# Second head's probability tiles turned by a DMA round over DRAM and VectorE's 32x32 transposes, with a new order of issue

## The chip, the cores and the metric

The kernel runs on one core of a Trainium2 chip. The metric is the device time of one execution in microseconds, from the program's start to its end. Five engines work side by side, each through its own list of instructions in the order in which they were issued: TensorE (matmuls and transposes, PE in the profile, PEld for its weight loads), VectorE (DVE), ScalarE (ACT), GpSimd (POOL) and SyncE (SP), which here only issues DMAs.

## The reference

Eight batches of eight heads of attention with a threshold, and a gated MLP behind it:

```python
# q, k, v: 8 x 8 x 576 x 64; x: 8 x 576 x 512
scores = scale * q @ k^T
thresh = max(scores, axis=-1) - tau
attn   = exp(where(scores >= thresh, scores, -1e9) - max); attn /= attn.sum(-1) + 1e-9
x      = heads of (attn @ v) side by side
h      = gelu(x @ w_in); u, v = halves of h
v_n    = (v - mean) / sqrt(var + 1e-6) * g_ln
gated  = u * (w_sg @ v_n + b_sg)
out    = x + gated @ w_out
```

## The kernel before, in words

Two heads make a pair, so there are 32 pairs, numbered n from 0, four a batch. A pair's 576 rows are cut into four tiles of 128 rows for each head and one tile that holds the last 64 rows of both. For each of the nine tiles TensorE makes the scores (L835, in a split of two float32r parts that adds up to full precision; L810 for pairs 0 to 3), VectorE takes the negated maximum (L844), GpSimd the threshold (L850), ScalarE the exponential (L871), and VectorE sets to zero what lies below the threshold and sums the row (L878). The result is the tile `p`, rows of queries by columns of keys, with head 0 in the first 512 columns and head 1 in the last.

The value product needs the keys on the partitions, so every 128x512 piece of `p` is turned: TensorE makes four 128x128 transposes into a PSUM bank (`transposes`, L538 by way of `turn`), with the data as weights and the identity as the moving operand, and ScalarE copies the bank into the tile `pt` (`place`, L1001). For pairs 4 to 30 head 1's four tiles go another way: a DMA copies the piece of `p` into a tile `m` of the type float32r (`move`, L887), and TensorE turns that (`turn_moved`, L541), where one pass an element is enough. The values then multiply `pt` in two parts of 256 and 320 columns (`values`, L1027), both heads into one bank. The row sums go through DRAM to lie along the columns (`ld`, L947 to L954), and VectorE scales (L1036).

Four finished pairs feed one batch's MLP: matmuls at L1126, each group of four followed by work of the other engines (L1105 to L1328), and a store (L1334).

What sets the order: all steps are collected in a list `plan`, and a table of numbers (`PLACES`) gives each step its place. A planner runs through the steps in that order with a price for each instruction and gives each PSUM result a free bank. The steps are then issued in that order, so each engine gets its instructions in it, and SyncE its DMAs, which it issues one after the other, each when what it waits for has come. A new DMA also waits for the eighth one before it. There are two rooms for `m`, two for `p`.

Of the kernel before, what the change touches and what calls it, by code (L numbers as in the profile page):

```python
# [14 lines left out]
F32 = mybir.dt.float32  # L15
# [19 lines left out]
PLACES = (  # L35
    "c-qZa3v^ZGmA>D9&b{ZJ`@YG2<^7NlNFWd1fdGO6Di&)Mb+lAkbzC#*npxAaUB#tst=h*b>ddqbOO{%7Xlt!)t!<}8+X@A-JmewBoA3q`z+iY9"
    "k~81_Pog|RAP^jna?id0+5f-y{`R*YCmzS~c-;Rx|H;k0cYf>q>TymHX#Yf@y-V5lQ+Ay4`N<y7NqbIRJxSO(d8w;yZSvDOb=${}Pdnwzr(Hkr"
    "oT|y`g|j_foZa5t?laH!^zdx-^4XqK?RF1z;G8aY#{O;=&h9{mp3}(Jjh=27y4BNmN(%JE{B!x^oZ*jidOGy79;XvG=ThkLoK4U9;^tg151dOI"
    "pC0++oR2@wNy5&>;&y5M=|w$V1n{&1;`AU-oll(yXX^2s<JgnCsB@NuGqSM@+`6LIxfS;yf1Dop(_=kd^36GCU+4xm=REm#0bxI@9?z$qKWE10"
    "Q>+KhS!jGlh@Fe$!8y$LT!cSe^=;>T)1@c=c+P@bw~6cYoClth>ZsFQy7YwC=fKVBQG7fX;?D()g*}=>x}V>ii>{;2X>;$HRr36QJKbRBUi&?#"  # L40
    "_ss6Eb3H#z!0ATBxxiDLi!tx4BA3*0ryIw6$5p4Ni=V3F=MT!IK=Cu`xaR_~Isc>E|Nk6!dg@2-z|g&h&t#5YiuixFbKG-*aqI=hdlHs&g4jFm"
    "IK7cmM!Tb4yD?!Oi<!z%cjIf<1&#(ni9VZ$s<Fzkec);W2mYbWOu=U#n_^7A_1fQmTV<jj-f0{d@_tS~3X~ywXmXpm3(0*+Zz?loYspZU@#c6="
    "!?aP;zJl2|KAJ!ArrKEYo7bSYZtB~0bp{YnkquA%=5YgA$VTGM2cNwoo`}FM#gfUp`-4|9g8Os(HI$k_Fp;{ad}O?Y+maYFX?R-{@FNPtGwwik"
    "IRyf@#~K0=e0ank2Q05DTmxSasV4ga8z$nhjj-VlBl}&OdMhJu!W%8ZAuJ8SXO6<c0yKgW3I9d}QH(bH7KobJ8Q_48GI@ks3bsFYgjNMhtaqrd"
    "IJgnVxNPRcRs%+v8MNNxG6vx9{OpU}sRcX&gR!gv%{0mM;R9F^1ta{E5Hc!}!fnq7fgJu<_T$3L(L)rs(%1~sAH%`$hkO>SP|K*>NEz7br@u&U"
    "rzLTozsly9zSxk9BL*#wU^hRLF!1XdlmiOp+CrjANz~T(9v8bqM$UR3S!{lQCcz|(1N=;Sfx~>L^05wf$jZ&e^9C$jjyG?>Vhf6R?xAcEPncz)"
    "K;mMh12m#U0pBZ&n@)T`mQAb9%+1=zXZ~C?nAA@Yp;qypJwz>%SYe!c2dxSLvj7c%54eIxFI0SVHU9Tb%%N<+Ux5XRo(-o*bG6Q#G!L5)&!SV`"
    "xi^2zHgfUuy<E3T@SdncDSh0`Z)TQ+Fqk4LJ}^KQuELvQEhZBfh7*x~ST`Df;$9!ETQB+w8KG6w1ytEzB#RC|cLf#PmbG?_(T-<ka^2?*H9-I^"
    "!H3wH=GQu`6%0^`4cJPJ-tpESZLwqmcKha8JauB=)oMPJp!dTv>Or2-YHd#nc%{KAa`@J#`ch9t>5Qki^yq9#hSO@JDW{AlOiet+?t^!A)GF0V"
    "oFIOIfn*jXbIP&R_pVq!(pXT8?Sg{097|;-hU3N|t622-cI5+`O7CKFmZpAlBMLEm3)cgwIO)ou55;CB3uXn@SpriHj;ie>oxci;X^9Gt!a@8G"  # L50
    "zeH{eJ$+5`4+<e425LP<ifr406nCWut&Qek@A&@6-(?Sb;cn|A3~!-Cuo!E2SRNVEtQc>^ZH60W5GC;qXk(?})5E3^p%N|L6=B*`hK>0=7N%hg"
    "#4>{%OK@YO)>A;P;?5`Q%jnOT^h3`uK3DCco_Gq|Buq@SEhH*kD`TJ}^YYLFN+3J|ztZs;g!R}%SN$XLRzgTmm7m8i6gOYSQm~ha2vqmkW7gtF"
    "*XE#P>&@vW9;2T7=1Lp_L_>DeVS_rTHR3pJi8FDUu}3K<Iu*Z^`1r?Q6W)%Ikkm6I@Or>(vr&tM25V^<WgC%8vC-IvDVRQaGS3)3V8)M0hg*bK"
    "-coHoh{|p(=iMmHo9~0(u@@)!J7Z#}{EpU>AdCt!)9_-I>@s3TiH?t5NQ8HwO2kSJB!Rc_5cLGE{JP*aPVzL&d^d&0g@F%rE`&?5K1|cpK*G2Q"
    "NEnluHOfFFg(GMMAEmIbH1q-$+N^T#2n0Dek=&@`lgw()#)JpQUkjssN_6^bhT~KivL1$}9n#b#Tn+dbSK>)R9?~gn)q|CiO`rmP>kY44*M<Za"
    "=sX>bH^jCYhHHb?lL%W1*-v~wg!>j27ytZU>Ceb!p>ay+MPAoa%WeU(Kr8kJhcQd(u^BCm%;%Xgqml{ycg3uqg5Q=wvO8n2?ijG`Fj{=Af|^Y("
    "sHy&$H<jVCE#<ZAucV$5zdT4w($klrB$w2kK#rzehy?=JZdxB%WAHkBt-eqtNjOJ^j@i@j>v0j*9p%L+{8h2L<{=PTP6VVL98oqFKE|g`W&aod"
    "g}7aQ#EpLgm%_a7GdGIHIHc|cQ4`t5PJ%$#?7LWajy}jvzV7FffI2(~FA*-NT(u+2_{5kutN01;Wm3bYUH6pexwm!8HQp2G$M_iD8Z6QN3}Mh&"
# [24 lines left out]
)
LAST_SCALE, SIGMA, SPREAD = 0.55, 1.155, 0.7
# [1331 lines left out]
```

## Time and profile before

| what | us |
|---|---|
| three timed runs | 961.38, 961.41, 962.68 (median 961.41) |
| the profiled execution, from its first to its last instruction | 959.4 |
| TensorE busy in it | 936.8 |
| VectorE, ScalarE, GpSimd busy | 663.8, 667.1, 564.4 |
| the sixteen DMA engines, share of the span | 45.6% |

For the profiled execution the profile gives the span alone; the median of the runs lies 2.0 us above it, which is what goes on around the first and last instruction. Busy time of TensorE is the union of its instructions, and these are pipelined: one begins before the one ahead of it has ended. How much room an instruction takes on TensorE is the distance from its start to that of the next. The share of busy time is a mean over stages; the pairs with moved tiles make one long stage in the middle, with the weights' preparation and pairs 0 to 3 ahead of it and the last batch's MLP behind it.

### The profile page before, as it was taken

Reading aid. Unit: us, or ns where it says so; the run is one execution under the profiler, and the core shown is the slowest. Engines: PE = TensorE matmul, PEld = TensorE weight load, DVE = VectorE, ACT = ScalarE, POOL = GpSimd, SP = SyncE. Lnnn points to the kernel's source line nnn. Section 1 sums busy time; section 2 is a strip of 40 time slices with the busy share of each in tenths; the row PEclk is TensorE's granted clock in tenths of the full one; section 3 lists DMA queues with packets and bytes.
Section 4 is the critical chain, followed back from the end, with each engine's and each line's share of the span. In section 5 each row is a group of like instructions: output and inputs, shape, how many; then the busy total and the mean of one; then the engine's idle time right before and its main releaser. Section 6 shows DMA issues by size and latency. Waiting matters only on the chain.

```text
span 959.4 us, 20206 instructions
## 1 busy us (share of the span) xinstructions
PE 936.8 (98%) x6822; PEld 800.2 (83%) x6822; DVE 663.8 (69%) x1407; ACT 667.1 (70%) x1395; POOL 564.4 (59%) x997
## 2 busy tenths in 40 slices
PE   7999999999999999999999999999999999999998
PEld 4555889987798888998888898888889888898898
DVE  7899975767777567666786568766677757765451
ACT  5987886767875677665777677766787567764552
POOL 5865665555644577446763557536675366644467
PEclk9999999999999999999999999999999999999999
DMA  8353145465545553555445554456535455341001
GB/s 299 111 143 99 61 123 148 149 185 158 149 129 151 158 147 118 136 162 167 136 133 158 153 153 141 133 142 185 156 119 153 141 160 155 98 127 52 20 7 50
DMA packets 75791, 128.74 MB, mean 134 GB/s; under 512 B 16948, under 2 KB 25383, under 8 KB 75688
## 3 DMA queue, kind: packets, MB, share of 16 engines
q1 hardware_dynamic: 75688, 127.45, 45.6%
q8 instruction: 54, 0.88, 0.4%
q14 instruction: 49, 0.40, 0.1%
HBM read 46.40 MB, written 9.56 MB: 58 GB/s over the span
## 4 chain that ended last, share of the span: by engine, by line
PE 77%; ACT 7%; DVE 7%; DMA 3%; POOL 3%; issue 2%; SPq 0%; POOLq 0%; DVEq 0%; ACTq 0%
PE all_banks L1126 36%; PE all_banks L1027 14%; PE all_banks L835 14%; PE all_banks L538 8%; PE all_banks L541 3%; ACT p L871 2%; DVE nm L844 2%; DVE p L878 1%; DMA m<-p 1%; ACT pt L1001 1%; POOL ot L1331 1%; DMA qz<-qhi 1%; PE all_banks L810 1%; DVE gt L1112 1%; ACT vv L1218 1%
## 5 line engine op out<-in xcount | busy, mean ns | idle before, releaser
L871 ACT ACTIVATE p<-all_banks,nm 128x576 f32<-128x576 f32 x256 | 184.6, 742 | 92.5 <-DVE nm L844 90.6
L844 DVE TENSOR_REDUCE nm<-all_banks 128x1 f32<-128x576 f32 x288 | 208.7, 751 | 52.5 <-PE all_banks L835 43.3
L878 DVE SCALAR_TENSOR_TENSOR p<-all_banks,nm,p 128x576 f32<-128x576 f32 x256 | 204.2, 813 | 48.3 <-POOL nm L850 27.2
L1001 ACT ACTIVATE pt<-all_banks 128x512 f32<-128x512 f32 (+1 forms) x320 | 163.9, 554 | 19.4 <-PE all_banks L538 11.4
L835 PE MATMUL all_banks<-ks,qst 128*128 128x288 f32 x560 | 157.1, 314 | 1.4 <-ACT pt L1001 0.6
L850 POOL TENSOR_TENSOR nm<-columns,nm 128x1 f32<-128x1 f32 x288 | 55.0, 195 | 147.6 <-DVE nm L844 134.5
L1027 PE MATMUL all_banks<-pt,rv 128*64 128x256 f32 (+1 forms) x1024 | 137.8, 411 | 0.0
L835 PE MATMUL all_banks<-kl,qz 128*128 128x288 f32 x448 | 123.6, 295 | 0.0
L538 PE MATMUL all_banks<-ident_r,p 128*128 128x128 f32 x720 | 115.7, 276 | 3.1 <-DVE p L878 2.3
L835 PEld LDWEIGHTS all_banks<-ks,qst 128*128 128x128 f32 x560 | 102.1, 188 | 14.6 <-issue 6.9
L1126 PE MATMUL all_banks<-wsh,z 128*128 128x288 f32 (+2 forms) x512 | 113.4, 298 | 0.3 <-DVE uu L1109 0.3
L1027 PEld LDWEIGHTS all_banks<-pt,rv 128*64 128x64 f32 x1024 | 69.5, 136 | 48.6 <-issue 6.1
L538 PEld LDWEIGHTS all_banks<-ident_r,p 128*128 128x128 f32 x720 | 84.9, 141 | 20.0 <-issue 6.5
L1126 PEld LDWEIGHTS all_banks<-wsh,z 128*128 128x128 f32 x512 | 85.1, 188 | 2.4 <-issue 1.4
L835 PEld LDWEIGHTS all_banks<-kl,qz 128*128 128x128 f32 x448 | 84.5, 189 | 0.2
L1126 PE MATMUL all_banks<-xh,wih 128*128 128x288 f32 (+2 forms) x256 | 77.0, 301 | 0.2 <-ACT ot L1328 0.2
L1126 PE MATMUL all_banks<-gh,woh 128*128 128x288 f32 (+2 forms) x256 | 76.6, 300 | 0.0
L1126 PE MATMUL all_banks<-xl,wih 128*128 128x288 f32 (+2 forms) x256 | 76.0, 297 | 0.0
L1126 PE MATMUL all_banks<-xh,wil 128*128 128x288 f32 (+2 forms) x256 | 75.8, 296 | 0.0
L1126 PE MATMUL all_banks<-gh,wol 128*128 128x288 f32 (+2 forms) x256 | 75.8, 297 | 0.0
L1126 PE MATMUL all_banks<-wsl,z 128*128 128x288 f32 (+2 forms) x256 | 75.7, 297 | 0.0
L1126 PE MATMUL all_banks<-gl,woh 128*128 128x288 f32 (+1 forms) x240 | 70.7, 296 | 0.0
(147 smaller groups left out, 2202.2 us busy)
## 6 DMA issues: line engine op xcount, KB each, us to landing
m<-p SPq DMA_DIRECT2D x108, 256.0 KB
rk<-in_kT SPq DMA_DIRECT2D x32, 320.0 KB
rv<-in_vP SPq DMA_DIRECT2D x32, 320.0 KB
ks<-khi SPq DMA_DIRECT2D x56, 160.0 KB
rq<-in_qT SPq DMA_DIRECT2D x31, 288.0 KB
qz<-qhi SPq DMA_DIRECT2D x56, 144.0 KB
qst<-qhi SPq DMA_DIRECT2D x56, 144.0 KB
qst<-rq SPq DMA_DIRECT2D x56, 144.0 KB
```

The costliest lines, as they stand in the source:

```text
L538: nc.tensor.transpose(out, x, ident_r.bitcast(F32))
L541: nc.tensor.transpose(out.bitcast(F32R), x, ident_r)
L810: nc.tensor.matmul(st["s", h, i][:, a, 0:HALF], st["q"][rows, qo:qo + P], st["k"][rows, lo:lo + HALF], start=True, stop=True)
L835: nc.tensor.matmul(sc[:, a, 0:HALF], w, x, start=(j == 0), stop=(j == len(terms) - 1))
L844: nc.vector.tensor_reduce(nmax, st["s", h, i][:, :, 0:HALF], AX.XY, ALU.max, negate=True)
L850: nc.gpsimd.tensor_tensor(thr, toff, st["nm", h, i], ALU.subtract)
L871: nc.scalar.activation(target(h, i), st["s", h, i][:, :, 0:HALF], AF.Exp, bias=st["nm", h, i])
L878: nc.vector.scalar_tensor_tensor(dst, st["s", h, i][:, :, 0:HALF], st["thr", h, i], dst, ALU.is_ge, ALU.mult, accum_out=st["l"][:, c:c + 1])
L1001: nc.scalar.activation(dst, src, AF.Copy)
L1027: nc.tensor.matmul(acc[h * D:(h + 1) * D, 0:w], st["v"][:, o:o + D], unit(h, a)[:, kt, 0:w] if kt < NM else tail_unit(a)[:, 0:w], start=(k ...
L1112: put("stt1", end, lambda: nc.vector.scalar_tensor_tensor(t["tmp"], t["tmp"], GELU_C, t["acc"], ALU.add, ALU.mult))
L1126: nc.tensor.matmul(st["acc"], *term(j), start=(j == 0), stop=(j == n - 1))
```

## The change

For pairs 4 to 30, head 1's four tiles are no longer moved and turned by TensorE and copied by ScalarE. Three steps take the place:

- `put_blocks`: a DMA writes the 128x512 piece of `p` to a DRAM tile `d` (four of them) as four groups of columns, so that each row of a partition goes out as four runs of 512 bytes.
- `get_blocks`: a second DMA reads it into `m` (128x512, again two rooms), so that partition 32g + j holds column group g of rows 4j to 4j + 3, in runs of 2 KB. The blocks of the grid thus lie on the partitions where their transposes belong.
- `turn_blocks`: one VectorE instruction turns the 32x32 blocks of `m` and writes straight into `pt`. It reads every fourth word, and writes every fourth word.

With that, partition r of `pt` holds the keys 4r to 4r + 3 in its four slices, not the keys r, 128 + r, 256 + r and 384 + r. So the values of these pairs are laid out to match (in `layout`, which prepares the inputs), and head 0's tiles and the tail tile, which TensorE still turns, take every fourth column of `p` for each transpose. The order of issue and the PSUM banks come from two tables now (`ORDER`, `FIRST_BANKS`), without the planner, whose classes are gone. The order of the steps differs all through the program.

```diff
-        moved = by_rows
+        turned = TURNED if by_rows else ()          # TURNED = (1,), Q = 32
...
-        def move(h, i):
+        def put_blocks(h, i):
+
+            def f():
+                st["d", h, i] = dram.tile([P // Q, P, P], F32, tag="d", name=f"d{n}_{h}_{i}", bufs=4)
+                nc.sync.dma_start(st["d", h, i].rearrange("g q c -> q g c"),
+                                  st["p", i][:, h * KW:h * KW + MAIN].rearrange("p (g c) -> p g c", g=P // Q))
+            return f
+
+        def get_blocks(h, i):
             tag = slot("m", ROOMS)
 
             def f():
-                st["m", h, i] = ppool.tile([P, MAIN], F32R, tag=tag, name=f"m{n}_{h}_{i}")
-                nc.sync.dma_start(st["m", h, i].bitcast(F32), st["p", i][:, h * KW:h * KW + MAIN])
+                st["m", h, i] = ppool.tile([P, MAIN], F32, tag=tag, name=f"m{n}_{h}_{i}")
+                nc.sync.dma_start(st["m", h, i], st["d", h, i].rearrange("g (j a) c -> (g j) (a c)", a=P // Q))
+            return f
+
+        def turn_blocks(h, i):
+
+            def f():
+                a, j = divmod(i, 2)
+                nc.vector.transpose(unit(h, a)[:, :, j * P:(j + 1) * P].rearrange("p c (j a) -> p a c j", j=Q),
+                                    st["m", h, i].rearrange("p (a k c) -> p a c k", a=P // Q, k=Q))
             return f
...
-                    if moved and i < NM and h:
-                        turn_moved(out, st["m", h, i][:, kt * P:(kt + 1) * P])
-                    else:
-                        turn(out, pt[:, o + kt * P:o + (kt + 1) * P])
+                    x = pt[:, o:o + MAIN]
+                    turn(out, x.rearrange("p (k c) -> p c k", c=NM)[:, kt] if turned else x[:, kt * P:(kt + 1) * P])
...
-            if moved and i < NM and h:
-                at("move", g, move(h, i))
-            at("t", g, transposes(h, i))
-            at("hi", g, place(h, i))
+            if i < NM and h in turned:
+                at("move", g, put_blocks(h, i))
+                at("fetch", g, get_blocks(h, i))
+                at("turn32", g, turn_blocks(h, i))
+            else:
+                at("t", g, transposes(h, i))
+                at("hi", g, place(h, i))
...
+    strided = vv[:, :, :, :main].reshape(b, h // 2, 2, P, main // P, d).transpose(0, 1, 3, 4, 2, 5)
+    for n in range(WHOLE_SCORES, b * h // 2 - 1):
+        vm[divmod(n, h // 2)] = strided[divmod(n, h // 2)]
...
-    planner = Planner()
-    tile_threshold_attention_gated_mlp(planner, *args, planner.rehearse, lambda name: BANKED)
-    order = planner.order()
+    order, banks = table()
+    banks = iter(banks)
```

Three places of pair 13 show what stands where. Names carry the pair first (`m13_1_3`: pair 13, head 1, tile 3). On SyncE, before, at the end of the pair:

```order
L887 DMA m13_1_2_4552<-p13_2_4510 128x512
L777 DMA qd_140<-qhi14_4416 64x64 x2
L757 DMA qz0_138<-qhi14_4416 64x576
L757 DMA qz1_139<-qhi14_4416 64x576
L887 DMA m13_1_3_4615<-p13_3_4591 128x512
L750 DMA ks14_1_4645<-khi14_4643 64x640 x2
```

and after (L606 is the put, L615 the fetch):

```order
L606 DMA d13_1_2_4524<-p13_2_4430 128x4x128
L477 DMA qz0_138<-qhi14_4292 64x576
L477 DMA qz1_139<-qhi14_4292 64x576
L615 DMA m13_1_1_4528<-d13_1_1_4403 128x512
L606 DMA d13_1_3_4530<-p13_3_4482 128x4x128
L615 DMA m13_1_2_4541<-d13_1_2_4524 128x512
L470 DMA ks14_0_4597<-khi14_4532 64x576 x2
L615 DMA m13_1_3_4600<-d13_1_3_4530 128x512
L470 DMA ks14_1_4619<-khi14_4532 64x640 x2
```

Each tile has two DMAs now, with some others between its put and its fetch, and the next pair's placements (`ks14`) stand behind a fetch.

On VectorE, before, from the pair's last selects to the next pair's first maximum:

```order
L878 SCALAR_TENSOR_TENSOR p13_3_4591,l13_4373<-all_banks_93,nm13_0_3_4609,p13_3_4591 128x576
L1112 SCALAR_TENSOR_TENSOR gtu2_0_0_4597<-gtu2_0_0_4597,all_banks_93 128x288
L878 SCALAR_TENSOR_TENSOR pm_141,l13_4373<-all_banks_93,nm13_0_4_4570,pm_141 128x576
L913 RECIPROCAL ir13_4634<-l13_4373 128x9
L1180 TENSOR_TENSOR vt2_4640<-all_banks_93,vt2_4640 64x512
```

and after (L598 is the select, L564 the maximum, L622 the block transpose):

```order
L598 SCALAR_TENSOR_TENSOR p13_3_4482,l13_4296<-all_banks_93,nm13_0_3_4489,p13_3_4482 128x576
L622 STREAM_TRANSPOSE pt13_1_0_4536<-m13_1_1_4528 128x4x4x32
L649 RECIPROCAL ir13_4559<-l13_4296 128x9
L917 TENSOR_TENSOR vt2_4543<-all_banks_93,vt2_4543 64x512
L846 SCALAR_TENSOR_TENSOR uu2_0_0_4564<-gtu2_0_0_4512,all_banks_93 128x288
L849 SCALAR_TENSOR_TENSOR gt2_4_4562<-gt2_4_4562,vt2_4543 64x512
L622 STREAM_TRANSPOSE pt13_1_1_4589<-m13_1_2_4541 128x4x4x32
L849 SCALAR_TENSOR_TENSOR gtu2_0_2_4585<-gtu2_0_2_4585,all_banks_93 128x288
L622 STREAM_TRANSPOSE pt13_1_1_4589<-m13_1_3_4600 128x4x4x32
L846 SCALAR_TENSOR_TENSOR vv2_4_4604<-gt2_4_4562,vt2_4543 64x512
L564 TENSOR_REDUCE nm14_0_0_4653<-all_banks_93 128x1
```

The last block transposes stand behind the pair's last select and ahead of the next pair's first maximum.

On TensorE, before, ahead of the pair's value products:

```order
L538 MATMUL all_banks_93<-ident_r_94,pm_141 128x128 x4
L538 MATMUL all_banks_93<-ident_r_94,ir13_4634 65x128
L541 MATMUL all_banks_93<-ident_r_94,m13_1_3_4615 128x128 x4
L1010 MATMUL all_banks_93<-both_103,pm_141 128x64
L1027 MATMUL all_banks_93<-pt13_0_0_4462,rv13_4413 64x256
```

and after (L261 turns, L863 is the MLP, L761 the value product):

```order
L261 MATMUL all_banks_93<-ident_r_94,p13_3_4482 128x128 x4
L863 MATMUL all_banks_93<-xh10_3697,wil2_114 128x288
L863 MATMUL all_banks_93<-xh11_4109,wih3_111 128x288
L863 MATMUL all_banks_93<-xl11_4111,wih3_111 128x288
L863 MATMUL all_banks_93<-xh11_4109,wil3_115 128x288
L261 MATMUL all_banks_93<-ident_r_94,ir13_4559 65x128
L761 MATMUL all_banks_93<-pt13_0_0_4414,rv13_4405 64x256
```

The transposes of `m` are gone, and the MLP's matmuls stand between the last transposes and the products.

## Rows read from the trace of the kernel before

**Rows 1.** The page's head: span; busy us (share of the span) by engine.

```profile
span 959.4 us, 20206 instructions
PE 936.8 (98%) x6822; PEld 800.2 (83%) x6822; DVE 663.8 (69%) x1407; ACT 667.1 (70%) x1395; POOL 564.4 (59%) x997
```

**Rows 2.** Three stretches: length, PE, PEld, DVE, ACT, POOL busy, clock, DMA share, GB/s.

```profile
0.00:106.00 106.00, 95.95 (x584) 59.05 (x584) 94.71 (x215) 85.25 (x184) 66.11 (x136) 0.98 0.46 147
106.00:860.00 754.00, 745.90 (x5567) 655.10 (x5566) 528.09 (x1109) 534.23 (x1106) 441.07 (x775) 1.00 0.51 146
860.00:959.40 99.40, 94.91 (x675) 86.09 (x673) 40.97 (x85) 47.62 (x106) 57.22 (x87) 1.00 0.10 33
```

**Rows 3.** Waits, all engines: who waited for whom, us, times, longest.

```profile
DVE nm L844 <- PE all_banks L835: 43.3, 57, 4.7
...
PE all_banks L541 <- DMA m<-p: 2.2, 3, 1.2
```

**Rows 4.** TensorE's timeline around transposes: start us, us, instructions.

```profile
448.14 0.80 PE L541 MATMUL all_banks<-ident_r,m 128*128 128x128 f32 x8
448.78 0.30 PE L538 MATMUL all_banks<-ident_r,p 128*128 128x128 f32 x1
...
449.05 0.29 PE L835 MATMUL all_banks<-kl,qz 128*128 128x288 f32 x1
449.18 0.29 PE L835 MATMUL all_banks<-ks,qst 128*128 128x288 f32 x1
...
454.15 0.46 PE L541 MATMUL all_banks<-ident_r,m 128*128 128x128 f32 x4
454.44 0.46 PE L1126 MATMUL all_banks<-wil,xh 128*128 128x512 f32 x1
454.74 0.40 PE L1126 MATMUL all_banks<-wih,xl 128*128 128x512 f32 x1
454.98 0.39 PE L1126 MATMUL all_banks<-wih,xh 128*128 128x512 f32 x1
...
456.35 1.03 PE L538 MATMUL all_banks<-ident_r,p 128*128 128x128 f32 x8
457.13 0.38 PE L1126 MATMUL all_banks<-gh,woh 128*128 128x288 f32 x1
...
459.36 0.46 PE L541 MATMUL all_banks<-ident_r,m 128*128 128x128 f32 x4
459.66 0.63 PE L538 MATMUL all_banks<-ident_r,pm 128*128 128x128 f32 x4
...
473.85 0.54 PE L541 MATMUL all_banks<-ident_r,m 128*128 128x128 f32 x4
474.22 0.46 PE L1126 MATMUL all_banks<-wih,xh 128*128 128x512 f32 x1
474.52 0.40 PE L1126 MATMUL all_banks<-wil,xh 128*128 128x512 f32 x1
```

**Rows 5.** Groups by line and form; the first for 106 to 860 us alone.

```profile
L1001 ACT ACTIVATE pt<-all_banks 128x512 f32<-128x512 f32 x214 | 122.4, 594 | 14.4 <-PE all_banks L538 7.0 <-PE all_banks L541 6.6
...
L1112 DVE SCALAR_TENSOR_TENSOR gtu<-gtu,all_banks 128x288 f32<-128x288 f32 x56 | 25.0, 446 | 21.5 <-ACT gtu L1105 21.1
L1112 DVE SCALAR_TENSOR_TENSOR gt<-gt,all_banks 128x512 f32<-128x512 f32 x32 | 21.7, 678 | 16.3 <-ACT gt L1105 16.2
L606 DVE TENSOR_SCALAR w<-room 128x512 uint32<-128x512 uint32 x8 | 5.8, 733 | 0.2
```

**Rows 6.** A piece of the chain; SyncE's timeline; the moves' DMA issues.

```profile
382.64 4.62 DMA m<-p
...
459.01 0.30 SPq L947 DMA_DIRECT2D ld<-ir  x1
460.31 0.47 SPq L952 DMA_DIRECT2D ir<-ld  x1
...
m<-p SPq DMA_DIRECT2D x108, 256.0 KB
```

More of the change, by code (lines that the diff above doesn't have):

```diff
@@ L3 @@
 from collections import namedtuple
-from contextlib import ExitStack, contextmanager
+from contextlib import ExitStack
 from functools import partial
@@ L107 @@
-BEGIN = 575.0
-DMA_ISSUE, DMA_ISSUE_PART, DMA_START, DMA_LANES, DMA_BYTES = 525, 690, 650, 8, 250.0
-WINDOW, WINDOW_BUSY, CLOCK, STREAM, PER_MATMUL = 10240 / 3, 3200 * P, 2.4, 2.333, 9.7
-RESHAPE = 165
-def time_of(engine, op, out, args, sums=False):
-    n = out.size // out.shape[0]
-    pointers = sum(a.size == a.shape[0] for a in args) if n > 1 else 0
-    args = args or [out]
-    half = out.shape[0] < P and n < 512
-    if op == "memset":
-        return n / 1.2 + (175 if engine == "gpsimd" and half else 35)
-    if engine == "tensor":
-        if op == "transpose":
-            return n * (1 if args[0].dtype == F32R else 2) / CLOCK + (8 if args[0].dtype == F32R else 2.3)
-        if args[0].dtype == F32:
-            return n * 4 / CLOCK * (0.5 if min(out.shape[0], args[0].shape[0]) < P else 1.0) + 4
-        return n / STREAM + PER_MATMUL
-    if engine == "scalar":
-        return n / 1.2 + (51 if args[0].psum else 93) + 93 * pointers + 115 * half
-    if engine == "vector":
-        fast = op == "tensor_scalar" and not args[0].psum
-        if op == "tensor_reduce":
-            n = args[0].size // args[0].shape[0]
-        elif op == "bn_stats":
-            n = args[0].size // args[0].shape[0]
-        return n / (1.92 if fast else 0.96) + 69 + (60 if pointers else 0) + (60 if sums else 0)
-    if engine == "gpsimd":
-        if n == 1 and op == "tensor_tensor":
-            return 464 if pointers else 150
-        if len(out.shape) == 4:
-            return 149 + n + 140
-        return 149 + n * (1.0 if op == "tensor_scalar" else 2.103) + (115 if half or 1 < n < 8 else 0)
-    if out.tile.dram:
-        return out.size * 0.44
-    return out.size * (4 if n >= P else 8) / DMA_BYTES
@@ L487, in bank @@
         k = bank_of(name)
[L488 removed]
+        return psum.tile([P, 512], F32, tag=k, name=name) if k == BANKED else all_banks[:, k, :]
     def two_banks(name):
         k = bank_of(name)
[L492 removed]
+        return psum.tile([P, 2, 512], F32, tag=k, name=name) if k == BANKED else all_banks[:, k:k + 2, :]
     ident_r = cpool.tile([P, P], F32R, name="ident_r")
@@ L538, in turn @@
         nc.tensor.transpose(out, x, ident_r.bitcast(F32))
-    def turn_moved(out, x):
-        nc.tensor.transpose(out.bitcast(F32R), x, ident_r)
     def warm_up():
@@ L1360, in tile_threshold_attention_gated_mlp, with table @@
     issue(plan)
+def table():
+    data = np.frombuffer(zlib.decompress(base64.b85decode(ORDER)), np.uint8).astype(np.uint16).reshape(2, -1)
+    order = np.cumsum((data[0] * 256 + data[1]).astype(np.int16).astype(int)).tolist()
+    banks = list(zlib.decompress(base64.b85decode(FIRST_BANKS)))
+    assert sorted(order) == list(range(len(order)))
+    return order, banks
 _INS = ["qT", "kT", "vP", "w_in", "g_ln", "w_sgT", "b_sg", "w_out"]
@@ L1412 @@
     with tile.TileContext(nc) as tc:
-        tile_threshold_attention_gated_mlp(tc, *args, issue, planner.bank_of.get)
+        tile_threshold_attention_gated_mlp(tc, *args, issue, lambda name: next(banks))
     r = run_bass_kernel_spmd(nc, [arrays], core_ids=[0])
```

375 lines of the change are left out of this document (87 added, 288 removed).

## Prediction, on record before the changed kernel ran

> **What bounds the kernel now.** I read the page's busy times and its split into stages first, then the list of waits, then TensorE's own timeline. TensorE is busy 936.8 of 959.4 us, VectorE and ScalarE some 70% each [rows 1], at a granted clock of 0.98 to 1.00 in all three stretches [rows 2]. The split shows where the change can act: the moved tiles all lie between 106 and 860 us, and there TensorE is busy 745.9 of 754 us, VectorE 528.1, ScalarE 534.2, and the DMA engines 51% [rows 2]. TensorE leaves 8.1 us idle in that stretch. Its waits are small and scattered; for a moved tile it waited 2.2 us in all, at three places [rows 3]. VectorE on the other hand waits for TensorE's scores [rows 3]. So TensorE's work sets the end, and work taken off it counts at nearly full price, as long as nobody else becomes late. A busy TensorE overlaps its own instructions, so I price by distances from start to start, not by durations.
>
> **What is removed from TensorE.** 27 pairs (numbers 4 to 30) times 4 tiles are 108 groups of four transposes of `m`. Five of these tiles stand in the timeline [rows 4]: from 454.15 to 454.44 a group takes 0.29 us, and the matmul behind it holds its place 0.30 instead of the usual 0.24 us, so 0.35; from 473.85 to 474.22 it takes 0.37; two groups together from 448.14 to 448.78 take 0.64; from 459.36 to 459.66 0.30. That is 1.66 us for five, 0.33 each, or 0.35 as the second case has a slower neighbour behind it too. 108 x 0.35 = **38 us** less TensorE work, all on the path that sets the end.
>
> **What is removed from ScalarE.** The 108 evacuations of 128x512 at 594 ns [rows 5] are 64 us: 534 becomes 470 us in the stretch. It is off the path, so I count it at nothing. It is cover for ScalarE's other work.
>
> **What is added to VectorE.** 108 block transposes of 128x512, from SBUF to SBUF. No such instruction is in the trace. The nearest rows are VectorE's 128x512 operations, 678 ns, and 733 ns for one with both sides in SBUF that writes every second word [rows 5]. Low end 0.68 us. The new operation reads and writes every fourth word, which no row shows; if each such word took two steps, then 512 steps more are to be paid, and 512 against 288 elements differ by 678 - 446 = 232 ns [rows 5], 1.04 ns an element: 0.53 us more, so 1.2 to 1.3 us at the high end. Both sides of nothing: it can't be free, as it is an instruction of its own on this engine. I take 0.7, since the row with every second word is close to the plain ones. 108 x 0.7 = 76 us: VectorE goes to 604 us of some 716, 84%; at the high end to 660 us, 92%. The Trainium skill (VectorE: DVE Perf Modes, section The three transpose paths) gives 311 ns for a 128x128 block grid in bf16; four of these would be an estimate of 1.24 us, my high end, and no run here shows it yet.
>
> VectorE isn't the bound at 84%, but everything in the attention queues behind it: the order of issue puts the four transposes of a pair between its last selects, and the next pair's maxima follow them. A transpose that waits for its fetch holds back those maxima, hence the exponentials, hence TensorE. I count 6 us for that, with 0 and 20 (at 92%) as ends.
>
> **What is added to the DMA queue.** One move a tile becomes a put into DRAM and a fetch. The longest piece that a move held on the chain is 4.62 us; a small write to DRAM held the fetch behind it for 1.30 us from start to start [rows 6]. One transfer more is thus 1.3 to 4.6 us. TensorE's four transposes (0.37) and the evacuation (0.59) go out of that path and the block transpose (0.7) comes in, so it grows by 1.0 to 4.4 us; I take 2.5. In the order of issue the matmuls between head 1's last scores of a pair and its first value product over the second part are worth 12.9 us a pair before and 13.5 after, each matmul priced by its distance from start to start (0.13 us for 288 columns [rows 4]). So each pair loses some 2 us of slack. That the waits for moved tiles were 2.2 us in 27 pairs [rows 3] says there is slack to lose; I count **5 us** of new waits, with 0 and 27 x (4.4 - 0.6) = 103 us (no slack at all) as ends. SP itself: a fetch waits there for its put, and loads and placements queue behind it, but on average five other issues stand between the two, about 0.5 us each, which is more than the low price of the landing. The engines' share: 28 MB more beside 146 GB/s x 754 us = 110 MB at 51% [rows 2, 6] gives some 64%, a little more for the short rows of the put; not a bound.
>
> **The strided reads by TensorE.** Head 0's and the tail tile's transposes, 27 x 20 = 540, now load every fourth word as weights. Four transposes of `m` start 0.29 us / 4 = 73 ns apart, so a weight load of 128 adjacent words takes no more than that; eight plain ones take 0.78 us, 98 ns apart [rows 4], so a load has 25 ns of cover. If a load doubles to 146 ns it shows with 48 ns: 540 x 48 = 26 us. The ends are 0 and 26; it can't gain, as count and shape stay. I take 0, because nothing in the trace (8-byte steps on VectorE at 733 against 678 ns) shows words at a distance costing double.
>
> **New order elsewhere.** Ahead of 106 us TensorE idles 10 us and behind 860 us 4.5 [rows 2]; the new order touches both. I take 0, with 10 gained and 5 lost as ends.
>
> **Sum.** Against the profiled execution's 959.4 us: -38 + 6 + 5 + 0 + 0 = -27, a span of 932. The median of the runs, 961.41, lies 2.0 above the span, so **934 us**, 2.8% less.
>
> **Rivals.**
> - *Dear block transposes.* Each takes 1.2 us, VectorE is at 92% of a 716 us stretch, and TensorE waits for maxima: -38 + 20 + 5 = -13, 948 us. For it: no row has four-word steps. Against it: ScalarE is relieved by 64 us.
> - *Every word from a line of its own, on TensorE too.* Weight loads of 146 ns give 26 us back; with the rest of the sum 960, with dear block transposes as well 970. For it: 98 ns leave only 25 of cover. The Trainium skill (SBUF — State Buffer, section Door 1: The DMA port swizzle) speaks of 16-byte lines and a penalty for each access that crosses to a new one; four words are 16 bytes. By that rule this case would be the forecast; the trace has no access of that step, so it has only the chance below.
> - *The round lands late* (this one ends slower). Two landings in a row take nearly the 4.62 us of the longest piece each, the transposes of the last tile stand waiting at VectorE, and TensorE waits before the value products. It decides at 38 / 27 = 1.4 us of new TensorE waiting a pair; at 2 us a pair it is 27 x 2 - 38 = +16, 977 us. For it: the pieces of 4.6 us are there, and DMA traffic grows by a quarter. Against it: the order gives every pair over 8 us of matmuls between those scores and products.
> - *All of it covered*, no new waits, and the order fills some of the idle time at the ends: -38 - 4, 919 us. For it: 8.1 us of idle time in 754 show that such an order can be found.
>
> **How the numbers follow.** Forecast (924 to 944) 0.45; dear block transposes 0.18; dear weight loads 0.14, half of them at or above the time before; late round 0.10; all covered 0.13. The likeliest gives 934. From 918 to 963 leaves out the late round and the worst of the weight loads, together some 0.17. A measurement of this kernel tells 0.2% from no change. Faster: 0.45 + 0.18 + 0.13 + 0.02 = 0.78, less a little for what I haven't seen, 0.77; same 0.06; slower 0.17.
>
> **What would show it.** The row of the block transposes: 0.7 us right, 1.2 the first rival. Head 0's transposes: starts still near 98 to 109 ns apart, or near 150. TensorE's waits for VectorE and for value products in the middle stretch: some 20 us in all is right, over 50 is the late round. VectorE's share there near 84%, ScalarE's near 65%. The forecast is wrong if TensorE's busy time in the stretch doesn't fall by some 38 us, or falls and comes back as waits before the products.

## The result, and the profile of the changed kernel

| kernel | median, us | lowest to highest | ratio to before, 95% interval |
|---|---|---|---|
| before | 962.04 | 961.38 to 963.25 | |
| changed | 946.46 | 944.31 to 946.81 | 0.9833, 0.9819 to 0.9847 |

The change takes 15.6 us off, 1.7%. The prediction was 934.0 with a range of 918 to 963: the time is inside the range, but 12.5 us above the forecast and just outside the forecast's own 924 to 944. It is next to the first rival's 948, *dear block transposes*.

The head of the changed kernel's page has the span and each engine's busy time; its answer is in [rows 1].

```profile
span 944.7 us, 19388 instructions
PE 919.3 (97%) x6390; PEld 777.6 (82%) x6390; DVE 758.7 (80%) x1515; ACT 613.3 (65%) x1287; POOL 562.5 (60%) x997
```

TensorE has the 432 transposes of `m` less (6822 to 6390), but its busy time fell by 17.5 us only. VectorE rose by 94.9 us, ScalarE fell by 53.8. By stages (length, then PE, PEld, DVE, ACT, POOL busy, granted clock, DMA share, GB/s), against [rows 2]:

```profile
0.00:106.00 106.00, 97.49 (x599) 62.55 (x600) 96.49 (x223) 86.84 (x187) 66.11 (x136) 1.00 0.48 150
106.00:860.00 754.00, 741.56 (x5229) 642.46 (x5230) 626.58 (x1219) 485.09 (x1013) 443.96 (x782) 1.00 0.66 184
860.00:944.70 84.70, 80.26 (x567) 72.61 (x563) 35.62 (x75) 41.40 (x90) 52.43 (x80) 1.00 0.09 29
```

In a stretch of fixed length a busy engine stays busy, so the gain has to be read from the counts. By 860 us TensorE had started 5828 instructions; before it was 6151, of which 432 were the transposes of `m`, so 5719 others. It was 109 instructions ahead, and the last stretch is 14.7 us shorter for it. VectorE was busy 83% of the middle stretch, 70% before.

The row that decides the case is that of the new instruction (group by line and form: busy us, mean ns; then the engine's idle time ahead of it and what ended it):

```profile
L622 DVE STREAM_TRANSPOSE pt<-m 128x512 f32<-128x512 f32 x108 | 122.7, 1147 | 22.5 <-DMA m<-d 22.5
```

1147 ns, where I had taken 700 and named 1.2 us as the high end.

Where TensorE's time went can be counted from starts: each instruction is given the distance to the next one's start, summed by line. A wait thus counts for the instruction ahead of it. Transposes of `m` 37.7 us before, none now. Against that the value products take 175.6 instead of 163.8 us, the MLP's matmuls 450.0 instead of 442.3, and all other transposes (L261, nearly all of `p`) 106.4 instead of 100.3, with the same number of instructions each. All else together is 2.4 us less. So 38 us are gone, and 26 of them came back in three places.

A place where it comes back can be looked at. This is TensorE's timeline at a pair's second products in the changed kernel (start us, us, instructions; in brackets the idle time ahead and who ended it):

```profile
453.58 0.29 PE L555 MATMUL all_banks<-kl,qz 128*128 128x288 f32 x1
453.80 0.75 PE L761 MATMUL all_banks<-pt,rv 128*64 128x320 f32 x2
455.42 1.57 PE L761 MATMUL all_banks<-pt,rv 128*64 128x320 f32 x10 [0.86 <-DVE pt L622]
```

VectorE's timeline there:

```profile
454.23 1.13 DVE L622 STREAM_TRANSPOSE pt<-m 128x512 f32<-128x512 f32 x1 [1.14 <-DMA m<-d]
455.26 1.37 DVE L564 TENSOR_REDUCE nm<-all_banks 128x1 f32<-128x576 f32 x2
```

And the chain of waits there (start us, us, what):

```profile
448.20 1.08 DVE pt L622
...
449.30 4.91 DMA m<-d
...
454.23 1.14 DVE pt L622
...
455.42 2.91 PE all_banks L761 x18
```

Head 0's first product runs at 453.80, head 1's has to wait for the last block transpose, which ends at 455.37; that one had waited for its fetch. The fetch in turn was issued at 449.30, 0.02 us after an earlier block transpose had ended and freed one of the two rooms of `m`: a longer block transpose also starts a fetch later. (Fetches waited 15.7 us in sum for such a room; with the shorter block transposes of `e_both` below, 7.6.) From first start to the next instruction's start, the 32 second products of the program take 100.8 us, 90.5 before.

### The profile page after: what moved, and what is told of

Same layout as the page of the kernel before. It is cut to its first block, busy times and chain, and to the rows that moved or that the text cites. A ratio compares the mean times of both kernels' runs of the same rounds, so it can differ in the third digit from the quotient of the medians.

```text
span 944.7 us, 19388 instructions
## 1 busy us (share of the span) xinstructions
PE 919.3 (97%) x6390; PEld 777.6 (82%) x6390; DVE 758.7 (80%) x1515; ACT 613.3 (65%) x1287; POOL 562.5 (60%) x997
## 4 chain that ended last, share of the span: by engine, by line
PE 39%; DVE 7%; POOL 5%; DMA 4%; ACT 4%; issue 3%; SPq 1%; POOLq 0%; ACTq 0%; DVEq 0%
PE all_banks L863 19%; PE all_banks L761 8%; PE all_banks L555 7%; PE all_banks L261 4%; DMA m<-d 2%; DVE pt L622 2%; DVE p L598 2%; DVE nm L564 1%; POOL ot L1068 1%; ACT p L591 1%; DMA qz<-qhi 1%; DVE vv L846 1%; POOL vv L958 1%; DVE bn L936 0%; ACT vv L955 0%
## 5 line engine op out<-in xcount | busy, mean ns | idle before, releaser
L564 DVE TENSOR_REDUCE nm<-all_banks 128x1 f32<-128x576 f32 x288 | 208.3, 749 | 33.9 <-PE all_banks L555 25.3
L598 DVE SCALAR_TENSOR_TENSOR p<-all_banks,nm,p 128x576 f32<-128x576 f32 x256 | 203.9, 811 | 28.9 <-ACT p L591 15.4
L761 PE MATMUL all_banks<-pt,rv 128*64 128x256 f32 (+1 forms) x1024 | 146.6, 412 | 3.1 <-ACT pt L735 1.6
L622 DVE STREAM_TRANSPOSE pt<-m 128x512 f32<-128x512 f32 x108 | 122.7, 1147 | 22.5 <-DMA m<-d 22.5
L261 PE MATMUL all_banks<-ident_r,p 128*128 128x128 f32 x720 | 124.3, 285 | 4.0 <-DVE p L598 1.4
L735 ACT ACTIVATE pt<-all_banks 128x512 f32<-128x512 f32 (+1 forms) x212 | 106.3, 530 | 27.5 <-PE all_banks L261 25.5
L261 PEld LDWEIGHTS all_banks<-ident_r,p 128*128 128x128 f32 x720 | 96.1, 181 | 27.6 <-DVE p L598 7.9
L761 PEld LDWEIGHTS all_banks<-pt,rv 128*64 128x64 f32 x1024 | 73.7, 136 | 54.5 <-issue 5.3
L555 PEld LDWEIGHTS all_banks<-ks,qst 128*128 128x128 f32 x560 | 102.7, 189 | 14.6 <-issue 5.0
L863 PE MATMUL all_banks<-wsh,z 128*128 128x288 f32 (+2 forms) x512 | 112.8, 298 | 0.9 <-ACT ir L679 0.6
L863 PEld LDWEIGHTS all_banks<-wsh,z 128*128 128x128 f32 x512 | 84.7, 188 | 1.6 <-ACT ir L679 0.8
L863 PE MATMUL all_banks<-xh,wih 128*128 128x288 f32 (+2 forms) x256 | 77.5, 303 | 1.2 <-DVE vv L846 0.9
L863 PE MATMUL all_banks<-gh,woh 128*128 128x288 f32 (+2 forms) x256 | 76.4, 300 | 1.0 <-DVE pm L598 0.6
L863 PE MATMUL all_banks<-xl,wih 128*128 128x288 f32 (+2 forms) x256 | 76.3, 298 | 0.0
L863 PE MATMUL all_banks<-xh,wil 128*128 128x288 f32 (+2 forms) x256 | 76.0, 299 | 0.0
L863 PE MATMUL all_banks<-gh,wol 128*128 128x288 f32 (+2 forms) x256 | 75.8, 299 | 0.0
L863 PE MATMUL all_banks<-wsl,z 128*128 128x288 f32 (+2 forms) x256 | 75.3, 297 | 0.0
```

Of the source, the lines that this page charges most:

```text
L261: nc.tensor.transpose(out, x, ident_r.bitcast(F32))
L555: nc.tensor.matmul(sc[:, a, 0:HALF], w, x, start=(j == 0), stop=(j == len(terms) - 1))
L564: nc.vector.tensor_reduce(nmax, st["s", h, i][:, :, 0:HALF], AX.XY, ALU.max, negate=True)
L598: nc.vector.scalar_tensor_tensor(dst, st["s", h, i][:, :, 0:HALF], st["thr", h, i], dst, ALU.is_ge, ALU.mult, accum_out=st["l"][:, c:c + 1])
L622: nc.vector.transpose(unit(h, a)[:, :, j * P:(j + 1) * P].rearrange("p c (j a) -> p a c j", j=Q), st["m", h, i].rearrange("p (a k c) -> p ...
L735: nc.scalar.activation(dst, src, AF.Copy)
```

## The experiments

All were timed in three rounds beside the kernel before, whose median lay between 961.3 and 962.0 each time. The changed kernel wasn't timed again beside them: differences from its 946.46 are differences of medians, and by the ratios to the kernel before they come out up to 1.2 us other (14.5 instead of 15.2 us for the first run). "Keys and rows in another order" in an expectation says which part of the computation differs.

### What makes a block transpose dear, and what that costs

`e_both` changes two patterns:

```diff
-                nc.vector.transpose(unit(h, a)[:, :, j * P:(j + 1) * P].rearrange("p c (j a) -> p a c j", j=Q),
-                                    st["m", h, i].rearrange("p (a k c) -> p a c k", a=P // Q, k=Q))
+                nc.vector.transpose(unit(h, a)[:, :, j * P:(j + 1) * P].rearrange("p c (a j) -> p a c j", j=Q),
+                                    st["m", h, i].rearrange("p (a c k) -> p a c k", a=P // Q, k=Q))
```

> The block transposes read and write words that lie next to each other instead of every fourth word; everything else is the changed kernel (the keys and the rows of head 1's turned tiles then stand in another order than the values', so these pairs' output is another). Theory A (what was lost of the 38 us are waits behind dear block transposes, 1147 ns each): if the step of four words is what makes them dear, one takes 600 to 750 ns, VectorE has 43 to 59 us less work, and the time falls by 8 to 12 us, to 934 to 938. Theory B (the DRAM round lands late), theory C (strided weight loads of head 0 and of the tail) and theory D (the new order of issue): the transposes may get cheaper, but the time stays within 1.5 us of 946.5. If the transposes stay at 1147 ns the step is not the reason for their price, and A is not tested.

Measured: 931.25 us, ratio 0.9682 (0.9667 to 0.9696), 15.2 us below the changed kernel. The row of the block transposes in `e_both`:

```profile
L622 DVE STREAM_TRANSPOSE pt<-m 128x512 f32<-128x512 f32 x108 | 74.4, 695 | 24.1 <-DMA m<-d 24.0
```

The busy times on its page:

```profile
PE 908.4 (98%) x6390; PEld 773.0 (83%) x6390; DVE 718.4 (77%) x1515; ACT 612.1 (66%) x1287; POOL 562.2 (60%) x997
```

The step of four words is the price: 695 ns without it. And the time follows, by more than the 8 to 12 us that I had expected. Theory A holds for these 15 us; the value products are back at 165.2 us by starts, the second ones at 91.8 (163.8 and 90.5 before).

`e_read` and `e_wonly` take one of the two patterns each.

> Only the read side of the block transposes takes words that lie next to each other, the write side keeps its step of four words (the keys of head 1's turned tiles stand in another order than the values'). If the price comes from the read side, 600 to 750 ns an instruction as with both sides; if from the write side, 1147 ns as now; if from both, half way, some 900 ns. Theory A: the time falls in proportion to what VectorE gains, about 0.2 us for each us of VectorE's work; B, C, D: no change within 1.5 us.

> Only the write side of the block transposes takes words that lie next to each other, the read side keeps its step of four words (the rows of head 1's turned tiles stand in another order). Durations as for the read side, the other way about: what the one run gains the other must not. Theory A: the time falls in proportion to what VectorE gains, about 0.2 us for each us of VectorE's work; B, C, D: no change within 1.5 us.

Measured: 942.51 us, ratio 0.9803 (0.9787 to 0.9820), and 945.71 us, 0.9830 (0.9805 to 0.9854). The row of the block transposes in `e_read`, with adjacent reads:

```profile
L622 DVE STREAM_TRANSPOSE pt<-m 128x512 f32<-128x512 f32 x108 | 119.0, 1117 | 17.6 <-DMA m<-d 17.5
```

The same in `e_wonly`, with adjacent writes:

```profile
L622 DVE STREAM_TRANSPOSE pt<-m 128x512 f32<-128x512 f32 x108 | 119.0, 1109 | 19.5 <-DMA m<-d 19.5
```

None of my three guesses held. A step on either side costs nearly the whole price (some 420 ns, 0.8 ns for each of the 512 words of a partition), and the second side adds 30 to 40 ns. Mending one side alone is worth little: 4 us at most, and nothing that can be told apart with the writes.

### Strided weight loads

```diff
-  turn(out, x.rearrange("p (k c) -> p c k", c=NM)[:, kt] if turned else x[:, kt * P:(kt + 1) * P])
+  turn(out, x[:, kt * P:(kt + 1) * P])
```

`e_weights` makes this edit in the changed kernel, `e_all` in `e_both`.

> Head 0's and the tail tile's transposes on TensorE load 128 columns that lie next to each other instead of every fourth one; everything else is the changed kernel (the keys of these tiles then stand in another order than the values'). Theory C (strided weight loads cost TensorE time): weight loads of these transposes fall from some 194 to 141 ns, their starts stand 109 instead of 120 ns apart, and the time falls by 6 us, to 940.5. Theories A, B, D: the loads get shorter beside other work, the time stays within 1.5 us of 946.5.

> Block transposes with adjacent words on both sides and, on top of it, adjacent weight loads for head 0 and the tail tile (keys and rows of the turned tiles in another order than the values'). Adjacent weights alone gave nothing (948.7), though the 720 loads fell from 197 to 140 ns. If that was because TensorE waits for VectorE anyway, they should show here, where TensorE is the bound again: 4 to 5 us below the run with adjacent block transposes alone, 926 to 927.5. If a longer weight load is hidden in any case, 931 with 1.5 us to either side.

Measured: 948.67 us, ratio 0.9868 (0.9847 to 0.9888), against 946.46 with strided loads; and 927.52 us, 0.9644 (0.9619 to 0.9670), against 931.25. The loads themselves in the changed kernel (shortest, median, longest ns):

```profile
L261 PEld LDWEIGHTS all_banks<-ident_r,p x720: 137/197/232, 12.8 to 889.8; 128*128 128x128 f32 x180
```

And in `e_weights`:

```profile
L261 PEld LDWEIGHTS all_banks<-ident_r,p x720: 137/140/231, 15.2 to 890.0; 128*128 128x128 f32 x180
```

The loads get 57 ns shorter, the transposes start 109 instead of 120 ns apart (medians), and TensorE spends 101.3 instead of 106.4 us on all of L261, as theory C says. But the time doesn't follow (940.5 was expected by theory C; the four runs of `e_weights` lie between 946.74 and 951.38): value products, scores, MLP matmuls and the weights' preparation are 5.4 us longer by starts. Theory C's price is right for TensorE and wrong for the kernel. In the kernel with cheap block transposes the same edit gave 3.7 us (the two intervals overlap slightly, so the size is rough). A reading that fits both is that what TensorE saves counts where TensorE is what is late.

### Latency or load

`e_last` makes both patterns adjacent for tile 3 alone, the tile that the second products wait for. `e_load` is `e_both` with VectorE work that nobody waits for:

```diff
   nc.vector.tensor_reduce(nmax, st["s", h, i][:, :, 0:HALF], AX.XY, ALU.max, negate=True)
+  if turned and not h and i < NM:
+      nc.vector.tensor_reduce(idle, g_bc[:, 0:360], AX.X, ALU.max)
```

> Of each pair's four block transposes only the last, tile 3's, reads and writes adjacent words (27 of 108; its keys and rows then stand in another order than the values'); the other 81 keep their step of four words. Two readings of what made the run with all 108 adjacent 15.2 us shorter. Latency: what counts is how soon the last turned tile of a pair is there, since the pair's products of 320 columns wait for it; then these 27 alone give most of it, the products of 320 columns get 6 to 8 us shorter in sum (98.0 to about 90), and the time is 936 to 939. Load: what counts is VectorE's time as a whole; then a quarter of the lightening gives a quarter of the gain, 3.8 us, and the time is 942 to 944.

> The kernel with adjacent words on both sides of all 108 block transposes (931.3 us), and on VectorE 108 added instructions that nothing waits for: behind the maximum of each of head 0's four tiles, in the same 27 pairs, a maximum over 360 words of a constant tile, some 0.45 us each, 48 us in all (about what the cheap transposes had saved). Load: VectorE's time counts wherever it is spent, at 15.2 us for 48.8 us, 0.31 us for each; the time goes back to 944 to 948. Place: only the time of the transposes themselves counts, since products wait for them; the time stays at 931 to 935.

Measured: `e_last` 941.73 us (939.79 to 944.41), ratio 0.9793 (0.9770 to 0.9816); `e_load` 951.72 us, 0.9896 (0.9863 to 0.9929). The busy times on the page of `e_last`:

```profile
PE 914.1 (97%) x6390; PEld 775.8 (83%) x6390; DVE 748.0 (80%) x1515; ACT 612.5 (65%) x1287; POOL 561.9 (60%) x997
```

Those of `e_load`:

```profile
PE 923.2 (97%) x6390; PEld 777.4 (82%) x6390; DVE 758.8 (80%) x1623; ACT 615.5 (65%) x1287; POOL 563.2 (59%) x997
```

And the instructions added in `e_load`, by line:

```profile
L567 DVE TENSOR_REDUCE idle<-g_bc 128x1 f32<-128x360 f32 x108 | 55.6, 515 | 0.0
```

`e_load` refutes the place reading. VectorE's busy time is back at that of the changed kernel (758.8 and 758.7 us), with cheap transposes and idle work, and the time is back too, 5 us above it even. In VectorE's busy time (a union, so less than the sum of durations) the three steps cost 0.38, 0.44 and 0.51 us for each us: `e_both` 15.2 us for 40.3, `e_last` 4.7 for 10.7, `e_load` 20.5 for 40.4. The runs of `e_load` lie 7 us apart (947.38 to 954.42), so the three are alike only roughly.

`e_last` is divided between the readings. Its time is load's, 0.3 us below the 942 to 944; the latency reading wanted most of the 15.2 us, and it gave a third. Its second products are shorter by what latency said, 93.9 instead of 100.8 us (the expectation's 98.0 for the same sum is 100.8 by this count).

TensorE's time by starts, us, in the profiled execution of each:

| | before | changed | `e_both` | `e_last` | `e_load` |
|---|---|---|---|---|---|
| transposes of `m` | 37.7 | 0 | 0 | 0 | 0 |
| other transposes | 100.3 | 106.4 | 102.7 | 105.2 | 106.9 |
| scores | 183.5 | 184.3 | 183.9 | 186.0 | 188.8 |
| first products, 256 columns | 73.3 | 74.8 | 73.3 | 74.9 | 73.8 |
| second products, 320 columns | 90.5 | 100.8 | 91.8 | 93.9 | 96.4 |
| MLP | 442.3 | 450.0 | 448.6 | 449.9 | 456.1 |
| the rest | 25.8 | 22.6 | 23.7 | 24.0 | 23.7 |
| all | 953.5 | 939.0 | 924.2 | 933.8 | 945.6 |

Of the 14.8 us that `e_both` gains here, 9.0 are in the second products, where latency counts. Of the 21.4 us that the idle work costs, only 4.6 are there; 16.6 are in the MLP's matmuls, the scores and the transposes. So most of what the dear transposes cost stands in the products that wait for them, while VectorE's time costs in other places too. An added instruction also delays whatever stands behind it in VectorE's list, so these runs don't separate load from latency altogether.

### The DRAM round

```diff
-  nc.sync.dma_start(st["m", h, i], st["d", h, i].rearrange("g (j a) c -> (g j) (a c)", a=P // Q))
+  nc.sync.dma_start(st["m", h, i], kT[b, 2 * hp:2 * hp + 2, :, 0:MAIN].rearrange("h d s -> (h d) s"))
```

> The fetch into m reads 128 rows of 2 KB from an input that always stands in DRAM, at the same place in SyncE's list, and not the tile its own put has just written; the put stays as it is, and so do the block transposes with their step of four words (head 1's turned tiles hold other numbers). So a fetch no longer waits for its put: SyncE's 23.1 us of such waits go, and tiles land earlier. Theory B (the DRAM round lands late): VectorE's 22.5 us of waits for m shrink to under 5, and the time falls by 5 to 10 us, to 936 to 941. Dear transposes (A) and strided weights: the time stays within 1.5 us of 946.5, since the transposes stay at 1147 ns.

Measured: 947.79 us, ratio 0.9841 (0.9807 to 0.9874). SyncE's waits for the put are gone from the list, but VectorE's for `m` are not (waits: us in total, times, longest):

```profile
DVE pt L622 <- DMA m<-in_kT: 20.1, 12, 5.1
```

Half of theory B falls: that a fetch must wait for its put costs nothing that can be measured, with an interval of some 3 us to either side. The other half isn't tested, since the fetches still came late for 12 of 108 transposes, held back at SyncE by other things (18.7 us of waiting until a block transpose had freed a room of `m`). They come as late in `e_both` (24.0 us in the row above), which is 15 us faster. What these 20 us of waiting are worth stays open; a third room for `m` wasn't tried.

### The order of issue

Four runs touch the order. `v_pv` delays 16 products by one to three TensorE steps; `v_mix` gives tile 3 back to TensorE; `a_oldorder` has the new way to turn in the old order, `b_order` the old way in the new order. Their edits are in the order tables, so the expectations describe them; of `v_mix` the lines are

```diff
+            if i == NM - 1 and h in turned and n in MIXED:
+                at("none", g, lambda: None)
+                at("t", g, transposes(h, i))
+                at("hi", g, place(h, i))
```

> The changed kernel with another order at 16 places: a product that waited 0.2 to 1.6 us inside itself for a block transpose is issued one to three TensorE steps later (scores, transposes of the next pair), with its scaling behind it; nothing else is changed. Latency reading: TensorE does other work while the last tile is being turned, the waits inside the products (some 13 us in sum over all 20 places) shrink to under 5, and the time falls by 5 to 9 us, to 938 to 941. Load reading: the scores that were put ahead wait in their turn for VectorE to give their banks free, and the time stays within 2 us of 946.5.

> The changed kernel with one of head 1's four turned tiles, tile 3, back on TensorE: four transposes straight out of p (strided weights as head 0's) and ScalarE's copy, without put, fetch and block transpose for this tile, in 27 pairs; the copy stands where the block transpose stood in the order, the transposes a few steps ahead. Load: VectorE has 31 us less, worth 10 to 12 us at 0.31 to 0.39 us for each; TensorE has 27 times about 0.43 us more, 11.6 us, priced between nothing (5 us less gave nothing in this kernel) and 0.7 us for each (what adjacent weights gave in the kernel with cheap transposes): 935 to 944. If TensorE's own work were what bounds this kernel, the 11.6 us would be paid in full and VectorE's would give nothing: 956 to 959.

> The changed kernel's way to turn the tiles in the order of the kernel before: its table of places and its PSUM banks, a put where the move stood, the block transpose where the copy of the moved tile stood or later (at least 44 steps behind its put where the pair's products leave room), the fetch half way between. Theory D (the new order is part of the gain): the round and the block transposes come in the way of what stands there, products and maxima wait for them, and the time is 960 to 985, no better than before. If the order matters little, within 6 us of 946.5.

> The kernel before (move by one DMA, TensorE turns m, ScalarE copies) in the order of the changed kernel: its order table and PSUM banks, the move where the put stands, the transposes of m some 45 steps behind (a few steps ahead of where the block transpose stands), the copy 8 steps behind them, each with a bank that is free there. If the new order were better by itself, the time falls below the 961.4 of before, to 945 to 958. If the order belongs to its mechanism, as the run with the block transposes in the old order (1071.1) suggests, TensorE and ScalarE get work at places that were not laid out for it, and the time is 970 to 1030.

Measured: 991.40 us (ratio 1.0316, 1.0291 to 1.0341), 1003.81 (1.0445, 1.0420 to 1.0470), 1071.09 (1.1142, 1.1100 to 1.1185) and 1130.67 (1.1734, 1.1689 to 1.1780). One row of the waits of each shows who stood (us in total, times, longest). In `v_pv`:

```profile
DVE ir L768 <- PE all_banks L759: 35.1, 16, 5.5
```

In `v_mix`:

```profile
PE all_banks L760 <- ACT pt L734: 13.0, 6, 3.7
```

In `a_oldorder`:

```profile
DVE pt L604 <- DMA m<-d: 66.3, 39, 5.2
```

In `b_order`:

```profile
PE all_banks L844 <- ACT pt L719: 43.4, 24, 5.1
```

All four missed every range that I had given, on the slow side. In `v_pv` the scaling of the products stayed where it was in VectorE's list, but for four of the 16, so VectorE now stood waiting for the delayed products, 35.1 us where it had been 4.7, and what stands behind it in the list came later. Neither of my readings allowed for that. TensorE's mean granted clock was lower as well, 0.984 against 1.000, and its busy time 928.5 against 919.3 us, so a part of the 45 us may be the clock's; that wasn't separated. In `v_mix` the copy by ScalarE came late for the products, and VectorE's maxima waited 79.4 us for scores where it had been 25.3. That run doesn't tell what VectorE's time is worth against TensorE's, because it lost more by its order than either reading had at stake; it is inconclusive. The last two say that the order can't be had apart from the way of turning: each half alone is slower than both together, and than neither. How much of that is the order's and how much the places that I gave to the steps which the other kernel doesn't have, they don't separate.

## Why the prediction was right, and where it was off

- **38 us off TensorE.** Right: 37.7 us by starts, all gone. That it would count at nearly full price was not: 26 of it came back.
- **64 us off ScalarE, worth nothing.** Busy 53.8 us less over the program, 64% of the middle stretch; no run tested ScalarE by itself.
- **The block transposes, 0.7 us.** This is the step that failed. "I take 0.7, since the row with every second word is close to the plain ones" took a step of two words as evidence for a step of four. With adjacent words the 0.7 was right (695 ns), and the kernel with adjacent words runs 931.25 us, where the sum with 0.7 said 934. That it fits so well is in part luck: by starts 6.3 us of what comes back there are in the MLP's matmuls, 2.4 in the other transposes and 1.3 in the second products, while the sum had 11 us of waits for maxima and ahead of the value products and nothing else. With the step it is 1147 ns, near the high end, 1.2 to 1.3, that I had worked out from two steps a word. The estimate of 1.24 us that I took from the Trainium skill (VectorE: DVE Perf Modes, section The three transpose paths) came close for a reason that the runs don't bear out: four of its blocks with adjacent words take 695 ns here.
- **VectorE's waits, 6 us, or 20 at the high end.** VectorE came to 83% of the middle stretch; I had said 84% with cheap transposes and 92% with dear ones. The 92% was too high, because I added up durations (the 108 transposes last 124 us in sum, but VectorE's busy time rose by 94.9) and divided by a stretch that had lost all of the 38 us. The price in time was right: 15.2 us between the two cases by `e_both`, where the sum put 14. That VectorE's time is paid for at 83% is what `e_load` shows.
- **The round, 5 us.** Put and fetch land after 2.8 and 3.0 us (medians), inside my 1.3 to 4.6 for one transfer more; the fetch on the chain above took 4.91. Of the waits only those for the put are tested: nothing. The DMA share came to 66%, where I said 64.
- **Strided weights, 0, or 26 at the high end.** TensorE pays 6.1 us more for the transposes that it keeps. In this kernel's time that is nothing (948.67 without the step), in the kernel with cheap transposes some 3.7. I was right in the time by an error about TensorE. The price of a load was misread too: "takes no more than that" put it at 73 ns from starts, but a load of 128 columns lasts 141 ns in the trace before, and loads run beside the transposes ahead of them. With the step it lasts 197 ns and not twice as long, and starts are 120 ns apart, between my two signs (98 to 109, and 150). The rule that I weighed, the Trainium skill's (SBUF — State Buffer, section Door 1: The DMA port swizzle), that each access crossing to a new 16-byte line pays, agrees in direction with both rows: 140 to 197 ns for a load, 695 to some 1110 for a block transpose.
- **The order, 0.** It can't be checked as a term: the order exists for this way of turning, and neither can be taken alone.
- **What would show it.** That "TensorE's busy time in the stretch" falls by some 38 us was a bad sign to name: it fell by 4.3. The stretch has a fixed length and TensorE fills it; the count of instructions is what moves. TensorE's idle time with a named cause in the stretch came to some 11 us (8 before), not 20: most of what came back shows in the distances between starts only.

So the first rival's sum, -38 + 20 + 5, came within 2 us of the time, and its cause, block transposes of 1.2 us, is the one measured. It had 0.18 where the forecast had 0.45, so that the time lies in the range is owed to a range that took in this rival. Its path isn't borne out: it had TensorE waiting for maxima, but TensorE's idle time that ended with VectorE is 5.3 us in the middle stretch, 3.5 before, while the second products take 10.3 us more by starts. (The second rival's 970 "with dear block transposes as well" is a slip: -38 + 20 + 5 + 26 makes 974.)

The MLP's matmuls, 7.7 us longer by starts than before, are explained in part. Of their distances 18 are over 150 ns longer than the median of their form, 8.9 us in all, where before it was 8 with 3.3 us; most of these are waits of the instruction behind, for VectorE, ScalarE or a DMA. In the kernel with all words adjacent the MLP is still 6.8 us longer than before; why the new order has more such waits stays open.

No kernel faster than the changed one came out of this as a version to use. Adjacent words on both sides of the block transposes would be worth 15 us, with adjacent weights 19, but as they stand these runs compute something else: keys and rows lie in other places. A kernel for use would, as far as I can see, have to give the tail tile, which shares the values' layout, the same places of the keys, and to regroup the rows in the round. That was not built, and whether it would keep the 15 us is not shown.

## What to carry to other kernels

Price a strided access by a row with that very step, and where there is none, by the worse end; here one side with a step of four words cost as much as two. Before counting an engine's gain, ask which engine's list the others wait for: VectorE at 83% was still waited for, so that 5 us off TensorE at 97% were worth nothing that could be measured and 40 us off VectorE were worth 15. A busy share says neither; take instructions out, or put idle ones in, and time it. And a hand-set order belongs to the durations it was laid out for: shifting sixteen products by one to three steps cost 45 us, the lower clock that came with it included.

## What the runs showed of the hardware

- A block transpose of 128x512 f32 from SBUF to SBUF takes 695 ns with adjacent words, 1117 with a step of four words on the write side alone (`e_read`), 1109 with it on the read side alone (`e_wonly`), and 1147 with both. The price of the step is paid about once.
- A weight load of 128 columns at a step of four words takes 197 ns instead of 140 (`e_weights`), and consecutive transposes start 120 instead of 109 ns apart: most of it is hidden behind the transposes ahead.
- On VectorE, idle for a fifth of the span, 108 added instructions of 515 ns whose result nobody reads (`e_load`) lengthened the program by 20.5 us, 0.51 us for each us that VectorE's busy time rose.
